# Filling products on TensorE between the chunks of a cached attention: a new count per chunk

## The chip, the cores and the metric

One core of a Trainium2 chip. The metric is the device time in microseconds, as the median of several runs of the whole kernel.

## The reference

Two decode steps of attention over a cache, with one query per sequence, four sequences, D = 512, 32 query heads and Dh = 128, in bf16. A has 8 key heads, each for four query heads, and looks at the last 2048 positions of its cache. B has 32 key heads and looks at all 8192. The two results stand side by side in the output.

```python
# A: Hkv = 8, W = min(4096, max(256, Sk // 4)) = 2048
q = (x @ wq).reshape(B, Sq, Hq, Dh).transpose(0, 2, 1, 3)
k = jnp.repeat(k_cache[:, :, Sk - W:, :], rep, axis=1)
v = jnp.repeat(v_cache[:, :, Sk - W:, :], rep, axis=1)
p = softmax(einsum("bhqd,bhkd->bhqk", q, k) * Dh ** -0.5)
a = einsum("bhqk,bhkd->bhqd", p, v).transpose(0, 2, 1, 3).reshape(B, Sq, Hq * Dh) @ wo
# B: the same with 32 key heads of its own and all Sk = 8192 positions
out = jnp.concatenate([a, b], axis=-1)
```

## The kernel before

The work goes in chunks. A has eight, one per key head (c = 0 to 7). B has 32 (c = 8 to 39): one for each group of four heads `hq` and each sequence `b`, the sequences inside. In what follows a chunk of B is y = c - 8, so that y = 0, 4, 8, ... 28 opens a head group. A chunk of B has 256 tiles of 128 positions of K and as many of V, 8.4 MB each.

All loads are issued from SP's queue (SyncE), in the order of the chunks: K of a chunk (`dma_kB`), then V (`dma_vB`), and ahead of a group's first K its part of B's output weights (`dma_wos`, 0.5 MB). Each waits until its place is free: K of chunk y+1 for the transposes of the first half of chunk y (their tiles lie in the same place; the second half is copied aside by GpSimd, L440), V of chunk y+1 for the last products of chunk y with V. So the issue of V hangs on PE's (TensorE's) progress at the end of a chunk, the issue of K on its progress in the middle.

What a chunk of B does on PE, in the order of `whole_B`:

- `reorder`: 16 products with a matrix of zeros and ones bring the group's output weights into the order that is wanted; VectorE and ScalarE copy the result out of PSUM (`take_wol`, L866 and L868)
- `more_busy`, the filling products. They multiply the unit matrix by another constant into a place that is overwritten later; nobody reads the result
- `emit_T`: K's tiles are transposed in groups of eight (L519). The first of them waits for K, which GpSimd's queue passes on once it has landed (L85). VectorE and ScalarE copy each group to SBUF (L596, L594)
- `emit_S`: the transposed tiles times the queries give scores (L521), two groups behind the transposes
- maximum, exponent and sums, in two halves of the positions
- `emit_pv`: the products with V (L521, `po` and `tr`), then the normalization and the products with the output weights (`fin`)

PE's instructions of all 32 chunks of B are one loop over y in PE's program; `x` is that loop's register in `more_busy`, and `n` is zero there. The filling products are an inner loop whose body is `BUSYBODY` = 3 products, a round; the number of rounds is an expression of y:

```python
((y + 30) >> 5) - ((y + 3) >> 5)   # 1 at y = 2 to 28, else 0
```

times `MOREBUSY` = 3, plus 1. So before there are four rounds at y = 2 to 28, and one round elsewhere. The expression stands as the inner loop's end, and the end is compared with the counter after each round by PE's sequencer (in the profile PEldq, with register instructions FUSED_REGOPS and MOVE, and COMPARE_BRANCH, all at L961).

Of the kernel before, what the change touches and what calls it, by code (L numbers as in the profile page):

```python
# [35 lines left out]
QV = (0, 8, 16, 24, 30)  # L36
NBUSY = 0
BUSYBODY = 3
MOREBUSY = 3
FILL = (6, 3)  # L40

TRM0, BC0, L0, Q0, XT0 = 0, 256, 288, 320, 448
# [146 lines left out]
def bass_concat_heads__sliding_block_cached__mha_block_cached__decode_kernel(  # L189
# [45 lines left out]
    with ExitStack() as es:  # L235
# [711 lines left out]
        def more_busy(c):  # L947

            n = c - NCA

            def mm(e):
                return e.matmul(sc[:, 1, :], identb[:, :], sel4[:, :, :].rearrange("p r x -> p (r x)"), start=True, stop=True)  # L952

            def emit(e, x=0):
                if isinstance(e, _Record):
                    return mm(e)
                if isinstance(x, int):
                    for _ in range(BUSYBODY):
                        mm(e)
                    return None  # L960
                with nc.Fori(0, (((x + n + 30) >> 5) - ((x + n + 3) >> 5)) * MOREBUSY + 1, 1, engines=type(mybir.ALL_ENGINES)([mybir.EngineType.PE])):  # L961
                    for _ in range(BUSYBODY):
                        mm(e)
                return None

            sch.add("pe", emit, at=n)
# [159 lines left out]
```

## Time and profile before

| what | before |
|---|---|
| median of 3 runs | 1368.91 us (1368.7 to 1369.06) |
| the profiled execution | 1368.63 us |
| its span, first to last instruction | 1366.9 us |
| mean granted clock of TensorE | 0.984 |
| read from HBM | 587.21 MB, 430 GB/s over the span |
| PE, PEld busy | 1222.5 us (89%), 1127.1 us (82%) |
| DVE, ACT, POOL busy | 731.2 us (53%), 555.0 us (41%), 202.8 us (15%) |

Times in the views count from the first instruction. PE is TensorE's products, PEld its loads of weights, PEldq the instructions that its sequencer handles alone. The trace misses some records of products: of the filling ones it has 226 products and 339 loads, and each product has one load. "issue" is time in which an engine waited for nothing that the profile shows.

### The profile page before, as it was taken

The page shows a single profiled execution, that of the slowest core. Times are in us where ns is not written, and L with a number is a line of the kernel's source. Part 1 is how long each engine was busy: PE and PEld are TensorE (multiplying, and loading weights), DVE is VectorE, ACT ScalarE, POOL GpSimd, SP SyncE. Part 2 cuts the span into 40 slices and gives each one's busy share as a digit, 9 for nine tenths or more (in the row PEclk, how much of TensorE's full clock was granted, in tenths as well). Part 3 has the DMA queues.
Part 4 walks back from the last instruction along what each step waited for, and adds up shares of the span by engine and source line. Part 5 has one row for each costly group of instructions (what it writes and reads, how often), then busy time and mean ns, then how long its engine had stood idle before and what let it go on. Part 6 is the DMA issues. An engine that isn't in the chain of part 4 may idle for free.

```text
span 1366.9 us, 62986 instructions
## 1 busy us (share of the span) xinstructions
PE 1222.5 (89%) x27834; PEld 1127.1 (82%) x27951; DVE 731.2 (53%) x1495; ACT 555.0 (41%) x777; POOL 202.8 (15%) x84
## 2 busy tenths in 40 slices
PE   6688799989998999989999899989999899999998
PEld 5688798878888988878889888878898888888888
DVE  2575355545555555545555555545555555455555
ACT  2353344334344443433444444334444343344443
POOL 2000022222210222222101222221022222200000
PEclk9998899999999999999999999999999999999999
DMA  9999999999999999999999999999999999999998
GB/s 398 427 428 431 430 439 432 438 433 428 433 433 426 441 433 433 426 432 443 432 430 430 441 432 432 432 433 435 433 432 430 439 433 432 430 439 420 433 424 368
DMA packets 16772, 587.51 MB, mean 430 GB/s; under 512 B 1880, under 2 KB 2032, under 8 KB 4208
## 3 DMA queue, kind: packets, MB, share of 16 engines
q1 hardware_dynamic: 16720, 587.21, 99.7%
q8 instruction: 15, 0.25, 0.1%
q14 instruction: 5, 0.04, 0.0%
q10 hardware_dynamic: 32, 0.01, 0.0%
HBM read 587.21 MB, written 0.01 MB: 430 GB/s over the span
## 4 chain that ended last, share of the span: by engine, by line
DMA 64%; PE 32%; DVE 1%; issue 1%; ACT 1%; SPq 0%; POOLq 0%; ACTq 0%; DVEq 0%
DMA kv<-in_B_k_cache_dram 58%; PE tr L519 20%; PE sc L521 9%; DMA kv<-in_A_k_cache_dram 4%; DMA kv<-in_B_v_cache_dram 3%; PE tr L521 2%; PE po L521 1%; PE ms L521 0%; DVE sA L649 0%; ACT pba L748 0%; PE sc L952 0%; ACT kt L594 0%; PE fin L521 0%; DVE kt L596 0%; ACT pbb L718 0%
## 5 line engine op out<-in xcount | busy, mean ns | idle before, releaser
L519 PE MATMUL tr<-identb,kv 128*128 128x128 bf16 x8704 | 662.1, 221 | 60.2 <-POOLq L85 49.8
L596 DVE COPY kt<-tr 128x1024 bf16<-128x1024 bf16 x736 | 502.2, 691 | 320.9 <-PE tr L519 317.8
L519 PEld LDWEIGHTS tr<-identb,kv 128*128 128x128 bf16 x8704 | 511.7, 99 | 77.0 <-issue 68.7
L594 ACT ACTIVATE kt<-tr 128x1024 bf16<-128x1024 bf16 x352 | 359.3, 1023 | 457.0 <-PE tr L519 454.8
L521 PE MATMUL sc<-qq,kt 128*128 128x64 bf16 x8192 | 398.9, 192 | 11.4 <-DVE kt L596 9.5
L521 PEld LDWEIGHTS sc<-qq,kt 128*128 128x128 bf16 x8192 | 327.9, 98 | 18.5 <-DVE kt L596 12.7
L440 POOL COPY kv<-kv 128x4096 int32<-128x4096 int32 x54 | 192.9, 3602 | 988.2 <-DMA kv<-in_B_k_cache_dram 988.2
L718 ACT ACTIVATE pbb<-sc,negb 32x128 bf16<-32x128 f32 x256 | 137.9, 539 | 134.2 <-DVE negb L700 131.4
L521 PE MATMUL tr<-pbb,kv 128*128 128x64 bf16 x4096 | 137.1, 194 | 27.1 <-ACT pbb L718 25.5
L521 PEld LDWEIGHTS tr<-pbb,kv 128*128 128x128 bf16 x4096 | 132.4, 100 | 30.9 <-issue 28.6
L521 PE MATMUL po<-pbb,kv 128*128 128x64 bf16 x4096 | 135.1, 194 | 2.9 <-issue 2.4
L521 PEld LDWEIGHTS po<-pbb,kv 128*128 128x128 bf16 x4096 | 127.5, 98 | 4.0 <-issue 2.5
L866 ACT ACTIVATE wol<-tr 128x512 bf16<-128x512 f32 x32 | 19.1, 597 | 201.4 <-PE po L521 201.4
L952 PE MATMUL sc<-sel,identb 128*128 128x512 bf16 x226 | 67.7, 381 | 9.5 <-issue 5.2
L868 DVE CAST wol<-tr 128x512 bf16<-128x512 f32 x64 | 41.2, 686 | 54.7 <-PE tr L521 54.7
L952 PEld LDWEIGHTS sc<-sel,identb 128*128 128x128 bf16 x339 | 30.6, 98 | 46.6 <-issue 14.2
L725 DVE TENSOR_REDUCE rs<-pbb 128x4 f32<-128x512 bf16 x32 | 22.0, 686 | 50.1 <-ACT pbb L718 50.1
L798 DVE RECIPROCAL ib<-ms 128x8 f32<-128x8 f32 x32 | 6.7, 208 | 58.8 <-PE ms L521 58.8
L521 PE MATMUL tr<-wos,back 32*128 32x512 bf16 x384 | 34.8, 383 | 0.5 <-issue 0.5
L521 PE MATMUL po<-wos,back 32*128 32x512 bf16 x128 | 33.9, 385 | 0.0
L686 DVE TENSOR_REDUCE gm<-ms 4x4 f32<-4x128 f32 x72 | 19.8, 275 | 25.0 <-PE ms L519 25.0
L666 DVE TENSOR_REDUCE rh<-sc 128x4 f32<-128x512 f32 x32 | 22.1, 692 | 14.3 <-PE sc L521 14.3
(90 smaller groups left out, 490.1 us busy)
## 6 DMA issues: line engine op xcount, KB each, us to landing
kv<-in_B_v_cache_dram SPq DMA_DIRECT2D x10, 4096.0 KB, 25.2
kv<-in_B_k_cache_dram SPq DMA_DIRECT2D x7, 4096.0 KB, 21.7
kv<-in_A_k_cache_dram SPq DMA_DIRECT2D x8, 2048.0 KB, 15.7
kv<-in_A_v_cache_dram SPq DMA_DIRECT2D x8, 2048.0 KB, 16.9
kv<-in_B_k_cache_dram SPq DMA_DIRECT2D x6, 2048.0 KB, 27.1
kv<-in_B_v_cache_dram SPq DMA_DIRECT2D x3, 2048.0 KB, 30.9
kv<-in_A_wq_dram SPq DMA_DIRECT2D x1, 4096.0 KB, 12.4
kv<-in_B_wq_dram SPq DMA_DIRECT2D x1, 4096.0 KB, 22.8
```

Of the source, the lines that this page charges most:

```text
L440: sch.add("pool", lambda e, dst=dst, org=org: e.tensor_copy(dst, org), waits=[("T", s0 + ch["NG"] - 1)] if g == QC[0] else [])
L519: sch.add("pe", lambda e: e.transpose(o, l, r), waits, key)
L521: sch.add("pe", lambda e: e.matmul(o, l, r, start=start, stop=stop), waits, key)
L594: sch.add("act", lambda e: e.activation(dst, src, ACTF.Copy), waits=waits, key=("ev", s))
L596: sch.add("dve", lambda e: e.tensor_copy(dst, src), waits=waits, key=("ev", s))
L666: sch.add("dve", lambda e: e.tensor_reduce(out=dst, in_=src, axis=AX.X, op=ALU.max), waits=[("S", ch["s"] + (half + 1) * ch["NG"] // 2 - 1 ...
L686: sch.add("dve", lambda e: e.tensor_reduce(out=gm[0:C, m, 0:U], in_=src, axis=AX.X, op=ALU.max), waits=[key_of("trm", c, half)], key=key_o ...
L718: sch.add("act", lambda e, src=src, dst=dst, pp=pp, u=u: e.activation(dst, src, ACTF.Exp, bias=negb[pp, half, u:u + 1], scale=scale), wait ...
L725: sch.add("dve", lambda e: e.tensor_reduce(out=dst, in_=probs_of(c, half).rearrange("p j u -> p u j"), axis=AX.X, op=ALU.add), waits=[("ex ...
L866: sch.add("act", lambda e, u=u, o=o: e.activation(wol[:, u, :], o, ACTF.Copy), waits=[("reord", c, u)], key=("wol", c, u))
L868: sch.add("dve", lambda e, u=u, o=o: e.tensor_copy(wol[:, u, :], o), waits=[("reord", c, u)], key=("wol", c, u))
L952: return e.matmul(sc[:, 1, :], identb[:, :], sel4[:, :, :].rearrange("p r x -> p (r x)"), start=True, stop=True)
```

## The change

Two constants and the expression of the rounds. With y = 2 to 28 the inner loop now has five rounds, at y = 4, 8, 12, 16, 20 and 24 seven; at y = 0, 1, 29, 30 and 31 it has one, as before. `first` is 1 at those six values and 0 at all others: the first difference is 0 where y is divisible by four and -1 elsewhere, the second takes out y = 0 and y = 28, and the +33, the shift and the -16 turn 1 into 1 and 0 or less into 0.

```diff
@@ -36,7 +36,8 @@
 BUSYBODY = 3
-MOREBUSY = 3
+MOREBUSY = 4
+GROUPBUSY = 2
 FILL = (6, 3)
@@ -958,7 +959,9 @@
                     for _ in range(BUSYBODY):
                         mm(e)
                     return None
-                with nc.Fori(0, (((x + n + 30) >> 5) - ((x + n + 3) >> 5)) * MOREBUSY + 1, 1, engines=type(mybir.ALL_ENGINES)([mybir.EngineType.PE])):
+                y = x + n
+                first = ((y >> 2) - ((y + 3) >> 2) + ((y + 31) >> 5) - ((y + 4) >> 5) + 33 >> 1) - 16
+                with nc.Fori(0, (((y + 30) >> 5) - ((y + 3) >> 5)) * MOREBUSY + first * GROUPBUSY + 1, 1, engines=type(mybir.ALL_ENGINES)([mybir.EngineType.PE])):
                     for _ in range(BUSYBODY):
                         mm(e)
                 return None
```

## The prediction

> **What bounds the kernel now.** I read the page first, then the stages of the heads of B, then the chain of waits, then PE's timeline and its sequencer around the filling products. A chunk of B is numbered y = 0 to 31; the change touches y = 2 to 28.
>
> ```profile
> span 1366.9 us, 62986 instructions
> DMA  9999999999999999999999999999999999999998
> ```
>
> The transfers fill the whole span. The table by stage, cut at four starts of a chunk's transposes (y = 5 to 8), says so chunk by chunk (the columns after the length are busy time of the engines, then PE's granted clock, the DMA share and GB/s):
>
> ```profile
> 327.60:366.29 38.69, 35.29 (x810) 32.47 (x815) 20.82 (x41) 15.82 (x22) 7.14 (x2) 1.00 1.00 434
> 366.29:404.99 38.70, 35.30 (x810) 32.46 (x815) 20.83 (x41) 15.81 (x22) 7.14 (x2) 1.00 1.00 434
> 404.99:444.97 39.98, 35.30 (x810) 32.48 (x815) 20.82 (x41) 15.82 (x22) 7.15 (x2) 1.00 1.01 434
> 444.97:483.67 38.70, 36.84 (x810) 34.07 (x815) 20.84 (x41) 15.83 (x22) 7.14 (x2) 0.96 1.00 432
> ```
>
> Ordinary chunks take 38.70 us at a DMA share of 1.00. The stage that ends with the opening of a head group takes 39.98, because wos (0.5 MB) comes too. In the last row PE ran at a clock of 0.96 and was busy 1.5 us longer, and the chunk still took 38.70. So B now goes at the pace of the transfers, and PE has some slack. How much is to be read from one boundary. From the chain of waits, SP's timeline, and PE's timeline (start, length, what, and in brackets the idle before it):
>
> ```profile
> 338.04 28.08 DMA kv<-in_B_k_cache_dram
> ```
>
> ```profile
> 359.98 0.33 SPq L464 DMA_DIRECT2D kv<-in_B_v_cache_dram  x1
> ```
>
> ```profile
> 361.51 0.37 PE L521 MATMUL po<-wos,back 32*128 32x512 bf16 x1
> 362.05 2.54 PE L952 MATMUL sc<-sel,identb 128*128 128x512 bf16 x8 [0.16 <-issue]
> 366.29 1.51 PE L519 MATMUL tr<-identb,kv 128*128 128x128 bf16 x24 [1.71 <-POOLq L85]
> ```
>
> The fill is followed by 1.71 us in which PE waits for K of the next chunk, which lands at 338.04 + 28.08 = 366.12. The V behind it is issued at 359.98, that is 6.1 us before that K is through. What it needs to begin is bounded by the first big transfer of the page:
>
> ```profile
> kv<-in_A_wq_dram SPq DMA_DIRECT2D x1, 4096.0 KB, 12.4
> ```
>
> 4.19 MB at 434 GB/s are 9.7 us, so 2.7 lie before the first byte. PE can therefore be late by 6.1 - 2.7 = 3.4 us in all before the transfers idle. Ahead of the first chunk of a head group (y = 8) PE's timeline has a longer wait:
>
> ```profile
> 439.45 2.54 PE L952 MATMUL sc<-sel,identb 128*128 128x512 bf16 x8 [0.16 <-issue]
> 444.97 1.72 PE L519 MATMUL tr<-identb,kv 128*128 128x128 bf16 x24 [2.98 <-POOLq L85]
> ```
>
> **The change as products.** From the chain at y = 28, where nothing is waited for:
>
> ```profile
> 1219.88 0.59 PE sc L952 x2
> 1220.53 0.60 PE sc L952 x2
> ```
>
> A round of three products takes PE 0.65 us (the trace misses one record in three). The new counts: 5 rounds instead of 4 at y = 2 to 28, 7 at y = 4, 8, 12, 16, 20, 24, and still one round at 0, 1, 29, 30, 31. As products alone this is 0.65 us out of 1.71 of idle time, and 3 x 0.65 = 1.95 out of 2.98: covered by the wait for K. Without that cover it would be 20 x 0.65 + 6 x 1.95 = 25 us.
>
> **The change as register work.** The loop's end is an expression of y, and in the built program of the kernel before it is worked out anew after each round, on PE's sequencer: the counter's +1 and seven operations, two of them shifts, packed six (with both shifts) in one register instruction and two in another, then a branch. All of them, and then single ones by narrow windows (count, shortest/median/longest ns, first and last start):
>
> ```profile
> L961 PEldq FUSED_REGOPS  x226: 37/120/228, 121.6 to 1327.1; - x113
> L961 PEldq COMPARE_BRANCH  x113: 69/201/212, 122.0 to 1327.1; - x113
> ```
>
> ```profile
> L961 PEldq FUSED_REGOPS  x1: 197/197/197, 362.3 to 362.3; - x1
> ...
> L961 PEldq FUSED_REGOPS  x1: 37/37/37, 362.6 to 362.6; - x1
> L961 PEldq COMPARE_BRANCH  x1: 201/201/201, 362.7 to 362.7; - x1
> ...
> L961 PEldq FUSED_REGOPS  x2: 37/117/197, 362.9 to 363.2; - x2
> L961 PEldq COMPARE_BRANCH  x1: 69/69/69, 363.3 to 363.3; - x1
> ```
>
> 226 is two for each of 113 rounds. The large one takes 197 ns, 0.26 us to the next start with its gap of 0.06; the small one 37 ns, 0.1 to the next start; the branch 201 ns when taken. From large to large it is
>
> ```profile
> L961 PEldq FUSED_REGOPS  x8: 37/117/207, 361.0 to 363.2; - x8
> ```
>
> from 361.0 to 362.9 in three rounds, some 0.65 us with the starts rounded to tenths. So the sequencer's round is as long as the products' 0.65. There is no room in it: whatever the change adds per round lengthens the round.
>
> It adds much. The new end has the old one (with a factor of 4), `first` (five shifts and eight other operations), a multiplication and an addition more: 23 operations with the counter, 7 of them shifts, against 8 with 2. I cost this from the two rows. By size: at six to an instruction, 23 need four; two more at the large price give 0.65 + 0.52 = 1.17, and if the old small one fills up too, 1.33. By shifts: 197 - 37 over two shifts is 80 ns each; 7 x 80 + 4 x 37 + 4 x 60 = 950 ns in place of 350, so 1.25. I take R = 1.25 us per round, between the two. The bounds: 0.85 (two more at the small price) and 1.6 (three more large, and the small one large). A gain is excluded, as nothing is taken out of the round.
>
> [...]
>
> **The sum.** The next chunk's transposes stand behind the fill in the same queue. Where the sequencer comes to the fill is the row of the loop's register move:
>
> ```profile
> L961 PEldq MOVE  x1: 29/29/29, 399.6 to 399.6; - x1
> L961 PEldq FUSED_REGOPS  x1: 202/202/202, 399.7 to 399.7; - x1
> ```
>
> From the start of the transposes (366.29) to there it is 33.3 us, 0.1 more to the first register instruction; then n rounds of R, less 0.3 (the last branch isn't taken and no products follow it), plus about 0.3 for the two register instructions at the small price that make the semaphores' values and the first weights. So PE's own period is 33.4 + nR: before, 33.4 + 4 x 0.65 = 36.0, under 38.70. After: n = 5 gives 39.65, 0.95 above 38.70; n = 7 gives 42.15, 2.17 above 39.98. Then K waits for nobody: PE sets the pace, V's issue at the end of each chunk slips, and the transfers idle. Late in all: y = 2 and 3, 1.9; six groups of three ordinary chunks and one opener, 6 x (3 x 0.95 + 2.17) = 30.1; y = 28 has 39.65 against 39.98, nothing. 32.0 less the 3.4 of lead is 28.6 us. Written for any R: 142 R - 148.9, zero at R = 1.05, 7.1 us for each 0.05.
>
> After y = 28 there is one round per chunk, 33.4 + 1.25 = 34.7, so the end goes at the transfers' pace again and gives nothing back: their lost time is lost. ACT's and DVE's copies of the reordered weights (take_wol) need the products before the fill alone, and do not move. SP's K (L425) is issued from the middle of the transposes and slips with them. It had more room than V: issued at 338.04, 10.4 us after its chunk's start, while V holds the engines for half a stage, 19.3.
>
> The profiled execution took 1368.63 us (span 1366.9), 0.3 under the median. 1368.63 + 28.6 = 1397.2; on the median, 1397.5.
>
> **The rivals.**
> *The register work stays hidden: no change.* This holds while R is under 1.05, that is, if the additions per round come to under 0.40 us. For it: the added operations are cheap if it is something else in the large one that makes it large, and not their number or the shifts. Against it: then six operations of any sort cost 197, and two more such instructions are 0.52 already. The time would be 1368.9. 9 in 100.
> *Warm openers pay: faster.* In the row at 444.97 the clock fell after 2.98 us of idling and PE lost 1.5 us. With 1.51 us for the first 24 transposes elsewhere, the chain shows such slow starts at three more of the six openers:
>
> ```profile
> 288.89 2.58 PE tr L519 x24
> ...
> 757.15 2.74 PE tr L519 x24
> ...
> 913.22 2.29 PE tr L519 x24
> ```
>
>  Seven rounds close the idle time; if PE set the pace there, 4 x 1.5 = 6 us would be won: 1362.9. Decides if transfers are not the bound; the last row of the table by stage is against it (38.70 with the slow start). 2 in 100.
> *The clock falls in the longer fill.* The products would keep PE busy for 0.65 of 1.25 us. If that is too little, each chunk starts at the slow clock like the one at 444.97: 1.5 us more in 26 chunks, 39 us, 1436. Against it: 1.71 us of plain idling at 366.29 left the clock at 1.00, and the new gaps are 0.6. [...] 5 in 100.
> *The count comes out wrong.* `first` subtracts a larger number from a smaller one ahead of the +33. If that were held at zero, every chunk with five rounds would have seven, 40 rounds more: 50 us on top, 1447. 2 in 100.
>
> **How the numbers follow.** The forecast has 82 in 100, at 1397.5. Within it R from 1.085 to 1.395 gives 1374 to 1418; R outside that I hold for 1 in 40, so 80 of 100 lie in this range; no rival's own time does. About 0.2% (2.7 us) is what a measurement of this kernel can tell from no change. Slower by more: 82 + 5 + 2 = 0.89. Within: 0.09. Faster: 0.02.
>
> **What would show it.** Right: four register instructions per round on PE's sequencer, two of them at about 200 ns or more; rounds 1.2 to 1.3 us apart, with PE idle between threes of products for "issue"; no wait of the transposes on the POOL queue after y = 4; ordinary stages of 39.6 and openers of 42.1 with a DMA share near 0.97; V issued some 2.7 us or less before K is through. Wrong at the first step: rounds still 0.65 apart, or under 1.05. Wrong at the second: longer rounds, but a PE clock under 1.00 in every stage, or stages still of 38.70 with the transposes late.

## The result, and the profile after

The changed kernel takes 1405.95 us (median of five runs, 1405.72 to 1407.24) against 1368.86 before: 1.0273 times as long, 95% interval 1.0262 to 1.0284, or 37.1 us more. The profiled execution took 1405.72 us.

From the page of the changed kernel, the span and the shares of the chain that ended last; behind them the share line of the kernel before:

```profile
span 1404.0 us, 63602 instructions
...
PE 78%; issue 9%; DMA 6%; DVE 3%; ACT 2%; ACTq 0%; SPq 0%; POOLq 0%; DVEq 0%
```

```profile
DMA 64%; PE 32%; DVE 1%; issue 1%; ACT 1%; SPq 0%; POOLq 0%; ACTq 0%; DVEq 0%
```

The end used to hang on transfers for 64% of the way, now for 6%; PE took over with 78, and 9% is "issue", time in which the engine waited for nothing that the profile shows. The stages of one head group (y = 15 to 18, columns as in the prediction's table):

```profile
696.95:736.80 39.85, 35.89 (x812) 32.51 (x818) 20.82 (x41) 15.83 (x22) 4.97 (x2) 1.00 0.99 418
736.80:779.21 42.41, 37.09 (x817) 32.93 (x824) 20.82 (x41) 15.84 (x22) 8.51 (x4) 1.00 1.00 425
779.21:819.09 39.88, 35.90 (x813) 32.51 (x818) 20.82 (x41) 15.82 (x22) 7.80 (x3) 1.00 0.96 408
819.09:858.96 39.87, 35.88 (x813) 32.50 (x818) 20.83 (x41) 15.82 (x22) 7.07 (x3) 1.00 0.98 418
```

Ordinary chunks have gone from 38.70 to 39.85 us, the stage that ends with an opener (the second one here, seven rounds) from 39.98 to 42.41. PE was busy for only some 0.6 us longer than the 35.30 of before, at a clock of 1.00: it lost the time waiting. The transfers idle where the prediction had it, behind V's late issue: from 2 to 4 us after it (issue at 729.34, the stretch from 731.34 to 733.34) they moved 66 GB/s, at the same place in the kernel before (issue at 633.45) 492. Where PE waits, its timeline at the end of an ordinary chunk shows (three products a round, one of them unrecorded):

```profile
733.14 0.59 PE L953 MATMUL sc<-sel,identb 128*128 128x512 bf16 x2 [0.49 <-issue]
734.40 0.59 PE L953 MATMUL sc<-sel,identb 128*128 128x512 bf16 x2 [0.66 <-issue]
735.70 0.59 PE L953 MATMUL sc<-sel,identb 128*128 128x512 bf16 x2 [0.71 <-issue]
736.80 0.62 PE L520 MATMUL tr<-identb,kv 128*128 128x128 bf16 x8 [0.50 <-issue]
```

Between rounds PE stands still for 0.5 to 0.7 us on "issue", and the transposes too wait for "issue" and no longer for GpSimd's queue, that is, for K. PE's sequencer in the whole kernel, and then one round of it from 734.2 to 735.5:

```profile
L964 PEldq FUSED_REGOPS  x608: 96/200/262, 121.5 to 1366.8; - x152
L964 PEldq COMPARE_BRANCH  x152: 75/207/212, 122.5 to 1367.0; - x152
```

```profile
L964 PEldq FUSED_REGOPS  x2: 193/222/252, 734.2 to 734.4; - x2
L964 PEldq FUSED_REGOPS  x2: 200/226/252, 734.4 to 734.8; - x2
L964 PEldq FUSED_REGOPS  x1: 96/96/96, 735.1 to 735.1; - x1
L964 PEldq COMPARE_BRANCH  x1: 207/207/207, 735.2 to 735.2; - x1
L964 PEldq FUSED_REGOPS  x1: 193/193/193, 735.5 to 735.5; - x1
```

608 are four register instructions for each of 152 rounds. The counts are those of the change: 21 x 5 + 6 x 7 + 5 = 152. In one round the register instructions take 193, 252, 200 and 96 ns in this order, and with the gaps and the branch the round is 735.5 - 734.2 = 1.3 us. (The narrow rows repeat an instruction that runs across the window's edge.)

### The profile page after: what moved, and what is told of

Its sections match the earlier page's. It is cut to its first block, busy times and chain, and to the rows that moved or that the text cites. A ratio compares the mean times of both kernels' runs of the same rounds, so it can differ in the third digit from the quotient of the medians.

```text
span 1404.0 us, 63602 instructions
## 1 busy us (share of the span) xinstructions
PE 1237.4 (88%) x27912; PEld 1122.5 (80%) x28068; DVE 730.7 (52%) x1495; ACT 555.1 (40%) x777; POOL 202.8 (14%) x84
## 4 chain that ended last, share of the span: by engine, by line
PE 78%; issue 9%; DMA 6%; DVE 3%; ACT 2%; ACTq 0%; SPq 0%; POOLq 0%; DVEq 0%
PE tr L520 34%; PE sc L522 17%; PE tr L522 12%; PE sc L953 6%; PE po L522 5%; DMA kv<-in_A_k_cache_dram 4%; DMA kv<-in_B_k_cache_dram 3%; PE ms L522 2%; ACT pbb L719 2%; DVE kt L597 2%; PE fin L522 1%; PE ms L520 1%; DVE sA L650 0%; DVE oz L833 0%; DVE negb L701 0%
## 5 line engine op out<-in xcount | busy, mean ns | idle before, releaser
L953 PE MATMUL sc<-sel,identb 128*128 128x512 bf16 x304 | 90.9, 381 | 64.5 <-issue 63.1
L953 PEld LDWEIGHTS sc<-sel,identb 128*128 128x128 bf16 x456 | 34.3, 97 | 121.1 <-issue 96.8
L522 PE MATMUL tr<-wos,back 32*128 32x512 bf16 x384 | 34.8, 383 | 0.7 <-issue 0.5
```

The source lines that it names most:

```text
L522: sch.add("pe", lambda e: e.matmul(o, l, r, start=start, stop=stop), waits, key)
```

## The experiments

Theory A: the loop's end, worked out by PE's sequencer after every round, sets the length of a round, and the rounds make PE slower than the transfers. Rival B: it is the number of products. Rival C: it is the longer code in PE's loop over the chunks. The kernel before took 1368.53 us beside all of these.

**The end worked out once.**

```diff
+                pe = type(mybir.ALL_ENGINES)([mybir.EngineType.PE])
+                rounds = nc.alloc_registers("rounds", engines=pe)
+                nc.regs_mov(rounds, (((y + 30) >> 5) - ((y + 3) >> 5)) * MOREBUSY + first * GROUPBUSY + 1)
-                with nc.Fori(0, (((y + 30) >> 5) ... + 1, 1, engines=...):
+                with nc.Fori(0, nc.snap(rounds, engines=pe, donate=True, min_val=1, max_val=MOREBUSY + GROUPBUSY + 1), 1, engines=pe):
```

> The new counts (5 and 7 rounds of 3) and the whole new expression stay, but it is worked out once per chunk, ahead of the inner loop, into a register; each round then only adds one to its counter and branches. Theory A (register work in every round sets the pace): rounds fall back to the 0.65 us of their products, PE's period to about 37.9 us in an ordinary chunk and 39.1 in an opener, both under the transfers' 38.70 and 39.98, and the time to that of the kernel before, 1368.9 within 0.5 us. Rival B (it is the number of products): the counts are unchanged, so about 1406. Rival C (it is the longer code in PE's loop over the chunks): the code is as long as in the changed kernel, so about 1406.

Measured: 1368.47 us, ratio to before 0.9999 (0.9989 to 1.0009). The same 152 rounds, each with one short register instruction:

```profile
L967 PEldq ALU_OP  x152: 36/36/36, 122.2 to 1327.5; - x152
```

and an opener on PE's timeline (y = 8, 21 products, 14 of them recorded), with the stages that end and begin there:

```profile
439.26 4.48 PE L953 MATMUL sc<-sel,identb 128*128 128x512 bf16 x14 [0.34 <-issue]
444.59 1.51 PE L520 MATMUL tr<-identb,kv 128*128 128x128 bf16 x24 [0.86 <-POOLq L86]
```

```profile
404.61:444.59 39.98, 37.08 (x816) 33.35 (x824) 20.83 (x41) 15.83 (x22) 7.15 (x2) 1.00 1.00 433
444.59:483.29 38.70, 35.88 (x812) 32.77 (x818) 20.82 (x41) 15.82 (x22) 7.14 (x2) 1.00 1.00 434
```

All products in one run without a gap, and there are 0.86 us of waiting for K left. The whole loss is gone with the same products and the same operations in the code, so B and C fall. The stages show what the new counts do apart from their cost: the clock that was 0.96 after this opener is 1.00, PE is 1 us less busy (35.88 against 36.84), and the stage is 38.70 as before.

**Five rounds with the old expression.** One constant:

```diff
-MOREBUSY = 3
+MOREBUSY = 4
```

> The kernel before with MOREBUSY = 4 alone: five rounds at y = 2 to 28, openers too, with the old expression. Theory A: rounds of 0.65 us, three more products per chunk covered by the 1.7 us of waiting for K: 1368.9 within 0.5 us. Rival B: five rounds of 3 make up 15 of the 21 rounds' worth of products that were added in an ordinary group, so a good half of the 37 us, about 1390.

Measured: 1368.49 us, ratio 1.0 (0.999 to 1.001). Three more products in each chunk cost nothing.

**The shifts taken out of `first`.** It is 0 at every y here, so all chunks have five rounds:

```diff
-first = ((y >> 2) - ((y + 3) >> 2) + ((y + 31) >> 5) - ((y + 4) >> 5) + 33 >> 1) - 16
+first = ((y * 4) - ((y + 3) * 4) + ((y + 31) * 2) - ((y + 4) * 2) + 33) * 2 - 150
```

> The changed kernel with the five shifts of first replaced by multiplications (and other constants, so that first is 0 at every y): the same number of operations in the same four register instructions, five rounds at y = 2 to 28. Only 2 of the 7 shifts are left. If the price of a register instruction goes by how many operations it holds, a round stays at 1.28 us, ordinary chunks at 39.85 and the time at about 1368.9 + 20 x 1.15 + 2.8 - 3.5 = 1391. If it goes by the shifts (some 50 to 80 ns each), the round falls to 0.9 to 1.03 us, PE's period to 38.0 to 38.6, under 38.70, and the time to 1368.9 to 1370.

Measured: 1372.2 us, ratio 1.0031 (1.002 to 1.0043), between the two. One round's second and third register instruction, and two chunks:

```profile
L964 PEldq FUSED_REGOPS  x1: 174/174/174, 441.1 to 441.1; - x1
...
L964 PEldq FUSED_REGOPS  x1: 143/143/143, 441.3 to 441.3; - x1
```

```profile
406.23:445.40 39.17, 35.88 (x813) 32.52 (x818) 20.83 (x41) 15.82 (x22) 6.33 (x3) 1.00 1.01 437
445.40:484.58 39.18, 35.90 (x813) 32.52 (x818) 20.82 (x41) 15.83 (x22) 7.63 (x3) 1.00 0.99 430
```

174 in place of 252 with three shifts less, and 143 in place of 200 with two less: in these rows a shift takes some 27 ns more than a multiplication, not 50 to 80. So the shifts are the smaller part of the price (78 of 252 ns, and 57 of 200); what is left goes with the other operations, but the run does not tell their number from their kind. With five rounds a chunk takes 39.17 in place of 39.85, so the round is 0.136 shorter, which is five shifts by 27 ns. All chunks take 39.17 here, openers too: with a mean of (3 x 38.70 + 39.98) / 4 = 39.02 for the transfers, the lead evens them out, and 26 x 0.15 = 3.9 is about the loss.

**Rounds of six products.** The new expression in every round:

```diff
-BUSYBODY = 3
-MOREBUSY = 4
-GROUPBUSY = 2
+BUSYBODY = 6
+MOREBUSY = 2
+GROUPBUSY = 1
```

> The changed kernel's expression in every round, but rounds of six products: BUSYBODY = 6, MOREBUSY = 2, GROUPBUSY = 1, so three rounds (18 products) at y = 2 to 28 and four (24) in the six openers, one (6) elsewhere. More products than in the changed kernel, and the same register work per round. Theory A: the round is about 1.3 us, by its products and its register work alike; PE's period is 34.5 + 3 x 1.3 = 38.4 in an ordinary chunk and 39.7 in an opener, just under the transfers': 1368.9, at most 1372. Rival B: more products than the changed kernel's, 1406 or more. Rival C: the same code and three more products in the loop, 1406 or more.

Measured: 1368.57 us, ratio 1.0 (0.999 to 1.001). An opener, with 24 products (20 recorded) in one run:

```profile
439.66 5.13 PE L953 MATMUL sc<-sel,identb 128*128 128x512 bf16 x20 [0.16 <-issue]
445.16 1.51 PE L520 MATMUL tr<-identb,kv 128*128 128x128 bf16 x24 [0.38 <-POOLq L86]
```

More products than in the changed kernel, with about as long a register work per round (with a factor of 1 the multiplication falls away, and the last of the four instructions takes 36 ns in place of 96); six products take 1.29 us (the rounds of three in the run with eight cheap rounds start 0.647 apart) and cover it.

**How many dear rounds are free.** An expression nearly as long as the new one (`first` with other constants, 0 at every y, seven shifts in all; here too the last of the four instructions takes 36 ns), four rounds in one kernel and six in another:

```diff
-first = ((y >> 2) - ((y + 3) >> 2) + ((y + 31) >> 5) - ((y + 4) >> 5) + 33 >> 1) - 16
+first = ((y >> 2) - ((y + 3) >> 2) + ((y + 1) >> 5) - ((y + 4) >> 5) + 34 >> 2) - 8
-MOREBUSY = 4
+MOREBUSY = 3      # in the other kernel 5
```

> The kernel before's counts (four rounds at y = 2 to 28, openers too) with an expression as long as the new one, 7 shifts in it, worked out in every round: first = ((y >> 2) - ((y + 3) >> 2) + ((y + 1) >> 5) - ((y + 4) >> 5) + 34 >> 2) - 8, which is 0 at every y. The step that is tested is the threshold: with R = 1.26 PE's period is 33.5 + 4 x 1.26 = 38.5, just under the transfers' 38.70, so the dear rounds cost nothing: 1368.5 to 1369.5. If dear register work costs by itself, in every round that has it (108 rounds against the changed kernel's 147 at y = 2 to 28): some 70% of the 37 us, about 1395.

> The same expression with six rounds at y = 2 to 28, openers too. PE's period is 33.5 + 6 x 1.26 = 41.1 in every chunk against a mean of 39.02 for the transfers: 26 x 2.1 = 54 us more, some 1422.

Measured: 1368.6 us, ratio 1.0 (0.999 to 1.001), with four; 1421.78 us, ratio 1.0386 (1.0369 to 1.0403), with six. An opener with four dear rounds, and from the chain of waits two starts of transposes with six:

```profile
753.27 0.59 PE L953 MATMUL sc<-sel,identb 128*128 128x512 bf16 x2 [0.43 <-issue]
754.50 0.59 PE L953 MATMUL sc<-sel,identb 128*128 128x512 bf16 x2 [0.64 <-issue]
757.12 1.51 PE L520 MATMUL tr<-identb,kv 128*128 128x128 bf16 x24 [2.03 <-POOLq L86]
```

```profile
705.26 1.51 PE tr L520 x24
746.26 1.51 PE tr L520 x24
```

With four, PE has the same standstills of 0.4 to 0.6 us between rounds, but behind them K is still waited for, here 2.03 us; on the chain from 700 to 830 us the transposes that start at 717.14, 757.12 and 795.83 all follow a transfer of K, and the time stays that of before. With six, the chunks on the chain from 700 to 830 us take 41.0 us each, 2.0 above the mean of 39.02; 26 x 2.0 = 52 of the 53.3 us lost. A round is (41.0 - 33.48) / 6 = 1.25 us here (33.48 is worked out under "The sum" below).

**Eight rounds with the old expression.** `MOREBUSY = 7` in the kernel before.

> The kernel before with MOREBUSY = 7 alone: eight rounds (24 products) at y = 2 to 28 with the old expression. Here the products themselves outgrow the wait for K: the fill begins 34.45 us after the transposes do, 24 products take 5.13, so PE's period is 39.6 in every chunk against a mean of 39.02: 26 x 0.56 = 15 us more, about 1383. Rounds are 0.65 us apart. If only register work could cost, 1368.9.

Measured: 1379.55 us, ratio 1.0078 (1.0061 to 1.0095). From the chain:

```profile
724.77 1.34 PE tr L519 x24
764.19 1.34 PE tr L519 x24
```

39.4 us per chunk: here products alone do cost, as they outgrow the wait for K. But 24 of them exceed the mean of 39.02 by 0.4 us only, where the changed kernel's 15 dear ones exceeded 38.70 by 1.15. The estimate of 39.6 was 0.2 too long, since the transposes start while the last products run (behind the products the chain has 1.34 us of the first 24, and 1.51 where they wait: 0.17 lies under the products); hence 11 us and not 15.

## Why the prediction was right

**The bound.** It held from y = 2 to 28: the kernel before goes at the transfers' pace, and the change made PE the slower of the two. The four kernels at 1368.5 to 1368.6, with 12 to 24 products a chunk and clocks of 0.98 to 0.99, show that neither the products nor the clock mattered as long as K was still waited for.

**The products** at nothing: shown by the end worked out once (1368.47 us) and by five cheap rounds (1368.49).

**The round, R = 1.25.** Measured: ordinary chunks and openers differ by two rounds, (42.41 - 39.85) / 2 = 1.28. Four register instructions were right, though in the built program they hold 22 operations and not 23, as y + 3 is worked out once for both differences. Of the two ways that led there, the one by size is the nearer: three instructions of 193 to 252 ns, and the small one grew to 96. The one by shifts had the price wrong, 80 ns each with all else nearly free, against some 27 above a multiplication; its sum came out near only because it charged to the shifts what the other operations cost.

**The sum, 28.6 us; measured, 37.1.** Three terms were mis-sized. R: 142 rounds by 0.025 are 3.6. The constant of PE's period: 39.85 - 5 x 1.275 = 33.48 and not 33.4, 26 chunks by 0.08 are 2.1. And y = 28, which I had at nothing, from the chains of waits of the two kernels, before and then after:

```profile
1185.41 1.51 PE tr L519 x24
...
1222.42 1.34 PE tr L519 x24
```

```profile
1222.70 1.51 PE tr L520 x24
...
1262.55 1.51 PE tr L520 x24
```

K of y = 28 comes in two halves, and before the transposes did not wait for it: that chunk came 37.01 us after the last and not 39.98. Now it is 39.85, 2.8 more, so PE is 40.1 late there.

A fourth step was wrong in kind: that the end goes at the transfers' pace again and gives nothing back. The chains behind y = 28, before and then after:

```profile
1257.30 1.49 PE tr L519 x24
1267.72 25.50 DMA kv<-in_B_k_cache_dram
1293.39 1.51 PE tr L519 x24
...
1326.15 34.18 DMA kv<-in_B_v_cache_dram
```

```profile
1262.55 1.51 PE tr L520 x24
...
1297.60 1.49 PE tr L520 x24
...
1332.62 1.49 PE tr L520 x24
...
1367.63 1.49 PE tr L520 x24
```

Before, PE waited there for K of y = 30 and for the last of V. After, no transfer is on the chain, and the chunks come at PE's own 35.0 us to the end. So 3.0 of the 40.1 came back: 1.1 at y = 30 (36.09 to 35.02) and 2.0 from the start of the last chunk (at 1328.5 and 1367.6) to the end (38.4 to 36.4), less 0.1 elsewhere. The lead of 3.4, which the prediction took off for the transfers, is another thing and was too small. V was issued 4.1 us before K was through (729.34, while GpSimd's copy that waits for K starts at 733.43), and not 2.7 or less. In the last 12 us of the span the transfers moved 172 GB/s against 257 before, so at 434 GB/s they were through 12 x (257 - 172) / 434 = 2.4 us earlier before the end, and thus 34.8 late, 5.3 less than PE at y = 28. That 3.0 lies near 3.4 is luck. In numbers: 32.0 + 3.6 + 2.1 + 2.8 = 40.5 for PE's delay, measured 40.1; less 3.0 it is 37.1.

**The rivals.** Hidden register work: it would have needed R under 1.05, and R was 1.28; with 1.14 in the kernel without shifts in `first`, 3.7 us were lost already. Warm openers: the clock did stay up, in the changed kernel (1.00 in all four stages) and with the end worked out once, where it won nothing (1368.47), as the transfers were the bound. A falling clock in the longer fill: not seen, 1.00 in the four stages. A wrong count: 152 rounds were run.

## What to carry to other kernels

A loop's end that is an expression can be worked out again on every turn, on the engine's own sequencer: here 608 register instructions for 152 rounds. With a body of three short products a turn lasted as long as the register work, 1.28 us against 0.65 for the products, and PE's busy time hardly showed it (35.89 us against 35.30, in stages of 39.85 against 38.70). Put such a value into a register once (1368.47 us here), or make the body long enough to cover it (1368.57), and look at the rows of the sequencer before adding operations to it. PE's slack per stage, 1.71 us of waiting in 38.70, told what was free here; past it every stage paid: 39.85 us with five dear rounds, 41.0 with six.

## What was not expected of the hardware

The time of a register instruction went by what the built programs hold in it: 37 ns with two operations on constants (before), 96 with three of which one adds two registers and 252 with seven and three shifts (after), 174 with seven and no shift (without shifts in `first`). Three shifts in place of multiplications are 78 of the 252 ns. Number alone does not explain the rest: where the end is worked out once, the shortest instruction is, by its size, the pair of operations of which one takes two registers, and it takes 72 ns, about twice the 37.

```profile
L966 PEldq FUSED_REGOPS  x128: 72/225/268, 121.1 to 1327.2; - x128
```

How much the number of operations costs by itself stays open. The loop's compare-and-branch took 201 to 213 ns when taken (medians of the kernels), and 69 to 82 when not (their shortest).
